# Idle matmuls in fp32, the first head group's norm taken in pieces, the second group's k moved off ScalarE, and a reordered start of the MLP, in an attention and MLP kernel

## The chip, the cores and the metric

One core of one Trainium2 chip. The metric is the time of one execution in microseconds (us), measured on the device. A profiled execution gives a trace as well. Its span is a little shorter than the timed duration (434.5 against 436.1 us for the kernel before). Stages are compared by spans, kernels by times. Each run of one core also lists the mean clock that TensorE was granted, as a share of full speed.

## The reference

Batch 8, 12 heads, 448 tokens, 64 numbers per head; then an MLP of 768 to 2048 to 768 on 3584 tokens. Everything arrives in fp32.

```python
def rmsnorm(x, g):
    return x / np.sqrt(np.mean(x * x, axis=-1, keepdims=True) + 1e-06) * g
q_n, k_n = rmsnorm(q, g_q), rmsnorm(k, g_k)
scores = np.matmul(q_n, k_n.transpose(0, 1, 3, 2)) / np.sqrt(64)
attn   = softmax(scores)                     # written out there: exp, sum, divide
x      = np.matmul(attn, v)                  # then (batch * tokens, heads * 64)
h      = x @ w_in
out    = (np.maximum(h, 0) + alpha * np.minimum(h, 0)) @ w_out
```

## The kernel before

The work is cut into 24 groups of four heads, three to a batch. The text counts groups from one; the code counts `y` from zero. A group goes through six steps:

1. `square` and `reduce` give the sums of squares, on ScalarE or GpSimd and then VectorE.
2. `root` makes the norm's factor of them, with two small operations on ScalarE.
3. `scale` multiplies q and k by the factors.
4. `turn` transposes both: on TensorE with a copy by VectorE for the first six groups (ScalarE copies the first q), by DMA later.
5. `score` makes seven tiles of scores, and `soft` takes the exponential of each on ScalarE.
6. `den` sums the exponentials over the keys on TensorE, `log` and `invert` make the reciprocal on ScalarE, `attv` multiplies with v.

Which engine does what, at the start:

```python
def square(y, nm):
    ...
    if y < 2:
        nc.scalar.activation(out=sqf, in_=src, func=AF.Square)
    else:
        nc.gpsimd.tensor_mul(out=sqf, in0=src, in1=src)

def scale(y, nm):
    ...
    eng = nc.vector if (y, nm) in ((0, "k"), (1, "q"), (2, "q"), (3, "q")) else nc.gpsimd
    eng.tensor_mul(out=..., in0=nat[y, nm], in1=...)      # rr, broadcast over a head

def spin(count):                                          # idle matmuls, fp16, 128 x 448
    if count:
        ps = psf.tile([128, 512], FP32, name="spin", tag="mm")
        for _ in range(count):
            nc.tensor.matmul(out=ps[:, :S], lhsT=ident, rhs=idle, start=True, stop=True)
```

In the traces each engine does its work in the order in which it is written here, so this order is the schedule. A "burst" is the two or three score tiles of one turn of the loop. `roots[n] = y` says after which burst the norm of group `y` is made. The burst with the second denominator is called `lead`; in it the first MLP steps (`up`) begin.

```python
spin(22)
...                                       # small transpose of the parameters
spin(6)
for nm in "qk":
    square(0, nm)
    reduce(0, nm)
...
for nm in "qk":
    root(0, nm)
    scale(0, nm)
...
turn(0)
square(1, "k")
load_v(0)
square(2, "q")
...
after(0, root, 1)
for nm in "qk":
    after(0, scale, 1, nm)
after(0, square, 2, "k")
after(0, load_w_in, 0)                    # GpSimd issues the first weights' DMAs
...
roots[3] = 2
for n in range(NB):
    ...
    if n in roots:
        y = roots[n]
        work = [(root, (y,)), (scale, (y, "q")), (scale, (y, "k"))]
        if lead:
            late = [(3, f, a) for f, a in work]       # after the third up step
        else:
            for f, a in work:
                f(*a)
    ...
    for k, (f, a) in enumerate(gaps[n]):              # the MLP steps of this burst
        ...
            f(*a, spare)
            done += 1
            if n in jobs and not (lead and done < 4):
                g, c = jobs[n].pop(0)                 # a reduce of the next group
                g(*c)
            if late and done == late[0][0]:
                for _, g, c in late:
                    g(*c)
                late = []
    ...
    if n < den_at[G - 1] - 1 and plain and n not in turns:
        spin(4)
```

## Time and profile before

| | before |
|---|---|
| time, median of 6 runs (range) | 436.12 us (435.75 to 436.34) |
| span of the profiled run, mean granted clock | 434.5 us, 0.995 |
| start of the first softmax (ScalarE) | 13.46 us |
| start of the first denominator (TensorE) | 28.40 us |
| start of the second denominator | 38.39 us |
| start of the turn of the fifth group | 52.95 us |
| start of the first down projection in a spare accumulator ("opa"), which is free only when VectorE has read the attention output of the fourth and fifth group out of it | 80.26 us |

The last five rows are milestones. They cut the span into six stages.

One more row of the page is needed later, the clock that was granted to TensorE, in tenths, 10.9 us to a digit:

```profile
PEclk9899999999999999999999999999999999999999
```

An undisturbed slice reads 9. The 8 in the second slice is one stretch of half clock, from 13.50 to 16.91 us. The record of the clock begins at 6.67 us, so the slow start before that is not in this row.

### The profile page before, as it was taken

The numbers are of one execution on the slowest core, as the hardware profiler recorded it, in microseconds if no ns is written. First come the engines' busy times: TensorE is split into PE (matmuls) and PEld (weight loads), VectorE is DVE, ScalarE is ACT, GpSimd is POOL, SyncE is SP. The second block draws the span as 40 slices with busy tenths as digits, with TensorE's granted clock in tenths as the row PEclk, the third lists the DMA queues.
The fourth block names the chain that finished last, engine by engine and source line by source line (L and its number), as shares of the span: only waits on it lengthen the run. The fifth ranks groups of instructions, "written<-read, shape, count | busy, mean of one in ns | idle before, by whom it ended". The sixth has DMA issues, their size and how long they took to land.

```text
span 434.5 us, 11509 instructions
## 1 busy us (share of the span) xinstructions
PE 417.4 (96%) x4977; PEld 215.9 (50%) x4977; DVE 204.9 (47%) x304; ACT 279.4 (64%) x385; POOL 175.8 (40%) x133
## 2 busy tenths in 40 slices
PE   7888799899999999999999999999999999999996
PEld 3344344354455445544555445554555545555564
DVE  3755564544554463546454463555453354233421
ACT  4997787588877577758757577757757587132300
POOL 5799792585373626074153636174133000000000
PEclk9899999999999999999999999999999999999999
DMA  8999999999668743968076752945082300211133
GB/s 186 234 234 218 166 210 175 201 174 189 158 104 178 170 107 62 203 101 195 20 137 156 156 129 55 200 101 121 20 150 48 80 4 21 55 38 28 28 72 75
DMA packets 70387, 53.85 MB, mean 124 GB/s; under 512 B 37424, under 2 KB 70336, under 8 KB 70336
## 3 DMA queue, kind: packets, MB, share of 16 engines
q1 hardware_dynamic: 55536, 40.19, 42.8%
q0 software_dynamic: 13984, 11.81, 18.3%
q10 hardware_dynamic: 816, 1.11, 1.1%
q8 instruction: 39, 0.64, 0.6%
q14 instruction: 12, 0.10, 0.1%
HBM read 45.62 MB, written 11.01 MB: 130 GB/s over the span
## 4 chain that ended last, share of the span: by engine, by line
PE 88%; DVE 4%; ACT 4%; issue 1%; DMA 1%; SPq 0%; ACTq 0%
PE op L364 28%; PE hT L326 21%; PE hTa L326 10%; PE sc L231 8%; PE opa L364 6%; PE dn L260 5%; PE av L260 5%; ACT expT L245 3%; PE avb L260 3%; DVE ss L153 2%; DMA nat<-in_k_dram 1%; PE tps L205 1%; DVE gT L354 1%; DVE osb L376 1%; ACT ah L353 1%
## 5 line engine op out<-in xcount | busy, mean ns | idle before, releaser
L245 ACT ACTIVATE expT<-sc,expb 128x896 f16<-128x896 f32 x168 | 161.6, 1005 | 38.8 <-PE sc L231 38.1
L364 PE MATMUL op<-w_out_sb,gT 128*128 128x384 f16 (+1 forms) x752 | 126.3, 323 | 0.0
L170 POOL TENSOR_TENSOR qs<-nat,rr 128x896 f16<-128x896 f32 x44 | 76.7, 1763 | 120.0 <-ACT rr L165 89.5
L364 PEld LDWEIGHTS <-gT 128*128 128x128 f16 x912 | 85.7, 98 | 64.8 <-issue 12.2
L326 PEld LDWEIGHTS <-w_in_sb 128*128 128x128 f16 x768 | 73.2, 98 | 74.9 <-issue 10.4
L326 PE MATMUL hT<-xT,w_in_sb 128*128 128x448 f16 x510 | 107.0, 353 | 2.0 <-DVE gT L354 2.0
L147 POOL TENSOR_TENSOR sq<-nat 128x896 f32<-128x896 f32 x44 | 73.4, 1683 | 39.9 <-DMA nat<-in_q_dram 29.1
L353 ACT ACTIVATE ah<-hT,cols 128x448 f16<-128x448 f32 x85 | 53.9, 635 | 44.0 <-PE hT L326 44.0
L354 DVE TENSOR_TENSOR gT<-hT,ah 128x448 f16<-128x448 f32 x85 | 52.8, 624 | 52.7 <-ACT ah L353 52.7
L376 DVE COPY osb<-op 128x384 f32<-128x384 f32 (+1 forms) x47 | 25.8, 549 | 90.5 <-PE op L364 90.5
L231 PE MATMUL sc<-qT,kT 64*32 64x448 f16 (+1 forms) x1092 | 54.0, 357 | 6.1 <-ACT expT L245 3.4
L153 DVE TENSOR_REDUCE ss<-sq 128x14 f32<-128x896 f32 x48 | 50.5, 1078 | 7.1 <-ACT sq L145 6.2
L326 PE MATMUL hTa<-xT,w_in_sb 128*128 128x448 f16 x246 | 53.2, 352 | 0.0
L353 ACT ACTIVATE ah<-hTa,cols 128x448 f16<-128x448 f32 x41 | 26.1, 635 | 31.2 <-PE hTa L326 31.2
L354 DVE TENSOR_TENSOR gT<-hTa,ah 128x448 f16<-128x448 f32 x41 | 25.6, 624 | 26.0 <-ACT ah L353 26.0
L231 PEld LDWEIGHTS <-kT 64*32 64x32 f16 (+1 forms) x1092 | 15.2, 93 | 37.3 <-issue 32.9
L364 PE MATMUL opa<-w_out_sb,gT 128*128 128x384 f16 x160 | 27.7, 326 | 0.0
L260 PE MATMUL dn<-expT,ones 64*32 64x448 f16 (+1 forms) x812 | 24.8, 350 | 2.6 <-issue 1.7
L311 DVE TENSOR_TENSOR xT<-av,rden 128x896 f16<-128x896 f32 x16 | 17.5, 1092 | 19.1 <-PE av L260 14.7
L260 PEld LDWEIGHTS <-vt 64*32 64x32 f16 (+1 forms) x1260 | 18.9, 94 | 13.2 <-issue 2.2
L260 PE MATMUL av<-expT,vt 64*32 64x448 f16 (+1 forms) x812 | 24.1, 349 | 0.0
L260 PEld LDWEIGHTS <-ones 64*32 64x32 f16 (+1 forms) x812 | 13.0, 94 | 12.6 <-issue 6.3
(43 smaller groups left out, 162.6 us busy)
## 6 DMA issues: line engine op xcount, KB each, us to landing
out_dram<-osb SPq DMA_DIRECT2D x109, 96.0 KB, 2.3
nat<-in_q_dram SPq DMA_DIRECT2D x46, 224.0 KB, 5.6
nat<-in_k_dram SPq DMA_DIRECT2D x46, 224.0 KB, 5.7
vt<-in_v_dram POOLq DMA_DIRECT2D x16, 336.0 KB, 6.4
w_in_sb<-in_moe_w_in_dram POOLq DMA_DIRECT2D x12, 256.0 KB, 7.4
w_out_sb<-in_moe_w_out_dram POOLq DMA_DIRECT2D x4, 768.0 KB, 11.5
nat<-in_q_dram ACTq DMA_DIRECT2D x2, 224.0 KB, 4.9
nat<-in_k_dram ACTq DMA_DIRECT2D x2, 224.0 KB, 6.3
```

What stands on the lines that cost most here:

```text
L147: nc.gpsimd.tensor_mul(out=sqf, in0=src, in1=src)
L153: nc.vector.tensor_reduce(out=ss_t[y][:, "qk".index(nm)].rearrange("p h j -> p (h j)").unsqueeze(2), in_=sqs[y, nm], axis=AXIS_X, op=ALU.add,)
L170: eng.tensor_mul(out=t.rearrange("p j h d -> p h j d"), in0=nat[y, nm], in1=rr_t[y][:, "qk".index(nm)].unsqueeze(3).broadcast_to((128, 2, ...
L231: nc.tensor.matmul(out=sc[ds(64 * g + m * c, m), par, :S].rearrange("p (j c) -> p j c", j=J), lhsT=kT[ds(64 * par, 64), j, g, ts(c, m)], r ...
L245: nc.scalar.activation(out=expT[y][:, j], in_=scs[y, j][:, :, :S], func=AF.Exp, scale=QK_SCALE, bias=expb[:, 0:1],)
L260: nc.tensor.matmul(out=accs[g][ds(m * h, m), :S], lhsT=weights(g, y, par, ts(c, m), j), rhs=expT[y][ds(64 * g, 64), j, par, :], start=(j = ...
L311: nc.vector.tensor_mul(out=x, in0=av[:, :, :S], in1=r)
L326: nc.tensor.matmul(out=hT[:, :S], lhsT=w_in_sb[:, g * G + i, ts(ft, 128)], rhs=xT[b][:, g, i, :], start=(i == 0 and g == 0), stop=(i == G ...
L353: nc.scalar.activation(out=ah, in_=hT[:, :S], func=AF.Copy, scale=alpha_sb[:, ft : ft + 1])
L354: nc.vector.tensor_max(out=gT[:, ft, ds((b & 1) * S, S)], in0=hT[:, :S], in1=ah)
L364: nc.tensor.matmul(out=ops[c][:, :PW], lhsT=gT[:, ft, ts(t, 128)], rhs=w_out_sb[:, ft, ds(oh * OH + c * PW, PW)], start=(ft == 0), stop=(f ...
L376: nc.vector.tensor_copy(out=o[:, ts(c, PW)], in_=ops[c][:, :PW])
```

## The change

The intent, part by part:

- **Idle matmuls.** They keep TensorE's clock up while it has nothing to do. Most become fp32, one wide one in place of four narrow ones, so that fewer instructions are needed.
- **First group.** q is squared, summed and scaled without waiting for k, by head halves; k is normed in two parts of its tokens (3/7 and 4/7). VectorE, not ScalarE, copies its turned q. The first softmax should start earlier.
- **Second group.** The square of its k moves from ScalarE to GpSimd, the scaling of its k from GpSimd to VectorE.
- **Third group.** Its norm is made one burst later (`roots[4]`), and on GpSimd the weights' DMA issues now stand ahead of the square of its k.
- **First MLP steps.** Both reductions of the next group go ahead of the first activation; one score tile and its softmax move behind the third and fourth `up`; the norms come after them.

The diff, cut to its core (the helpers that work on parts of the first group are left out; each is the operation of its name on a slice):

```diff
-    idle = gT[:, 0, :S]
+    idle32 = gT[:, 0, :].bitcast(FP32)
@@ square
-        if y < 2:
+        if (y, nm) == (1, "q"):
             nc.scalar.activation(out=sqf, in_=src, func=AF.Square)
@@ scale
-        eng = nc.vector if (y, nm) in ((0, "k"), (1, "q"), (2, "q"), (3, "q")) else nc.gpsimd
+        eng = nc.vector if y == 1 or nm == "q" and 0 < y <= G else nc.gpsimd
@@ spin
+                out=ps[:, :S], lhsT=idle32[:, :128] if wide else ident,
+                rhs=idle32 if wide else idle, start=True, stop=True,
@@ start
-    spin(22)
+    spin(3)
+    spin(18, False)
 ...
-    spin(6)
-    for nm in "qk":
-        square(0, nm)
-        reduce(0, nm)
+    spin(1)
+    for h in range(2):
+        part_square("q", slice(h, h + 1), full, nc.scalar)
+    for h in range(2):
+        part_reduce("q", slice(h, h + 1), full)
+    part_root("q", full)
+    part_scale("q", full, J, nc.gpsimd)
+    part_square("k", both, lo, nc.scalar)          # lo, hi: 3/7 and 4/7 of the tokens
+    part_square("k", both, hi, nc.scalar)
 ...                                                # reduce, root, turn, copy in parts
     square(1, "k")
+    reduce(1, "q")
+    square(2, "q")
     load_v(0)
-    square(2, "q")
+    after(0, part_turn, "k", range(K0, J))
+    after(0, part_copy, "k", hi, nc.vector)
+    after(0, reduce, 1, "k")
+    mid[1] = 1                                     # norm before the second burst's last softmax
     for nm in "qk":
-        reduce(1, nm)
-    after(0, root, 1)
-    for nm in "qk":
-        after(0, scale, 1, nm)
-    after(0, square, 2, "k")
-    after(0, load_w_in, 0)
+        after(1, scale, 1, nm)
+    after(1, load_w_in, 0)
+    after(1, square, 2, "k")
 ...
-    roots[3] = 2
+    roots[4] = 2
@@ loop
             if lead:
-                late = [(3, f, a) for f, a in work]
+                late = [(3, score, tiles[2]), (4, soft, tiles[2])]
+            if lead or wait and y < TD:
+                late += [(late[-1][0], f, a) for f, a in work]
 ...
-                if n in jobs and not (lead and done < 4):
+                if n in jobs:
 ...
-            spin(4)
+            spin(1)
```

## The prediction

> **What bounds the kernel now.** I read the page first, for the shares by slice; then the chain of work that ended last, in order of time; then the timeline of the first 57 us; then the table by stretches; last the waits of TensorE.
>
> ```profile
> PE   7888799899999999999999999999999999999996
> ACT  4997787588877577758757577757757587132300
> ```
>
> A slice is 10.9 us. From the sixth slice on TensorE is over 90% busy in nearly every one, and the table by stretches has it busy for 99.70 of the 100 us from 150 on. The change touches nothing after the third head group, so it can only pay in the first five slices, where TensorE is at 70 to 80%. There the chain shows who sets the pace:
>
> ```profile
> 7.51 0.96 ACT sq L145
> 8.49 1.10 DVE ss L153
> ...
> 10.20 1.44 DVE qs L170
> ...
> 11.68 0.58 PE tps L205 x7
> ...
> 12.29 0.70 DVE kT L216
> ...
> 13.46 1.91 ACT expT L245 x2
> ```
>
> The columns are start, length and work. This is a serial line from the arrival of k (7.5) to the first softmax (13.46). From then on ScalarE is nearly saturated:
>
> ```profile
> 15.78 5.67 ACT L245 ACTIVATE expT<-sc,expb 128x896 f16<-128x896 f32 x6
> 21.89 0.32 ACT L164 ACTIVATE rr<-ss,epsb 128x28 f32<-128x28 f32 x1 [0.44 <-DVE ss L153]
> 22.37 7.46 ACT L245 ACTIVATE expT<-sc,expb 128x896 f16<-128x896 f32 x8
> ```
>
> Eight softmaxes take 7.46 us (0.93 each); from 13.46 to 30.20, where the first denominator is logged, there are 16 of them (14.9) and three norms ("roots", 0.55 each): 16.6 of 16.74 us. So up to there the time is that of the first softmax plus stalls of ScalarE. A third stretch is the first MLP steps, where TensorE waits for a buffer that VectorE's reductions hold up:
>
> ```profile
> 47.94 1.07 DVE L153 TENSOR_REDUCE ss<-sq 128x14 f32<-128x896 f32 x1
> ...
> 49.60 1.29 PE L326 MATMUL hT<-xT,w_in_sb 128*128 128x448 f16 x6 [0.87 <-DVE gT L354]
> ...
> 50.58 0.32 ACT L164 ACTIVATE rr<-ss,epsb 128x28 f32<-128x28 f32 x1 [1.79 <-DVE ss L153]
> ...
> 52.63 0.38 PE L231 MATMUL sc<-qT,kT 64*64 64x448 f16 x4 [1.42 <-ACT expT L245]
> ```
>
> The brackets are idle time just before and its releaser: a reduction put between two activations delays the second (0.87 of TensorE), and ScalarE sits 1.79 us in front of the norm that needs the second reduction, so that the next softmax and scores are late (1.42).
>
> **What the Trainium skill says.** "TensorE: Matmul & The Clock Gate", Part 1 (the HAM clock gate): TensorE runs at half clock until one free-running window of about 3.4 us has been busy, and falls back after an idle one. The trace agrees: idle matmuls of 448 columns come every 0.37 us until 6.7, then every 0.19, and are back at 0.37 at 13.5 to 15.2. "FP8 and Floating Point Precision", TensorE Precision Notes: true fp32 takes four passes through the array. No line here shows it; I take one fp32 idle matmul as four fp16 ones (0.75 us, 1.5 at half clock). "SBUF — State Buffer", SBUF: two separate sides: VectorE and GpSimd share a port pair, and the one that starts second blocks for the whole instruction. The trace agrees:
>
> ```profile
> 8.99 1.69 POOL L170 TENSOR_TENSOR qs<-nat,rr 128x896 f16<-128x896 f32 x1 [4.68 <-ACT rr L165]
> 15.87 1.09 DVE L170 TENSOR_TENSOR qs<-nat,rr 128x896 f16<-128x896 f32 x1 [0.91 <-ACT rr L165]
> 15.91 2.60 POOL L170 TENSOR_TENSOR qs<-nat,rr 128x896 f16<-128x896 f32 x1 [0.56 <-ACT rr L165]
> ```
>
> The same scaling is 1.69 us alone on GpSimd, 2.60 beside one of VectorE.
>
> **The change, part by part.**
>
> *Idle matmuls.* At the start 22 + 6 narrow ones become 3 wide, 18 narrow, the small transpose, 1 wide: 30 narrow units before the transpose instead of 22. If the clock rises at 6.7 again: 14 units by then, 16 x 0.187 = 3.0, end 9.7; transpose 0.1 to 0.2 and the wide one 0.75: TensorE is free at 10.5. If it rises one or two us sooner, at about 9.7. Later bursts have one wide for four narrow: the same time.
>
> *First group.* q: two squares of 448 (0.57 each, from 0.95 for 896 with some 0.1 fixed) and two reductions follow its arrival at 5.5; sum ready at 7.2 and root at 7.8, no longer behind k's square. GpSimd scales q 7.85 to 9.54 (before 8.99 to 10.68). k: squares of 3/7 and 4/7 end 8.9, its second reduction 9.55, VectorE scales the first part 9.6 to 10.1, GpSimd the second 10.2 to 11.2. TensorE turns q at 9.7 to 10.5 and three blocks of k (0.8 together); VectorE copies q (0.62, was 0.91 on ScalarE) and 3/7 of k (0.36); scores 0.43. First softmax: 10.5 + 0.6 + 0.65 + 0.4 + 0.45 = 12.6, with the early clock 11.9. Against 13.46 that is 0.9 to 1.5 won. I take 1.2.
>
> *Second group.* k's square leaves ScalarE for GpSimd (0.95 us that lay before the first softmax, in the shadow of the turn), and both scalings run on VectorE, 2.2 in sequence, where GpSimd's blocked 2.60 ended before. Norm at about 15.2, scalings to 17.8, turns and copies to 19.2, against 19.87 before. TensorE turns k in order before it scores the next tile: about 0.3 us of stall.
>
> *Third group: its norm moves one burst later.* It now follows ten softmaxes instead of eight, but its turn stays where it was, so only two softmaxes are left between norm and first dependent tile, where there were four. Before, that tile's softmax came at 26.12, 3.65 us after the norm ended (22.47): GpSimd's blocked scaling 2.6, turn 0.55, scores 0.4. GpSimd still does this scaling and VectorE still starts beside it. So: first softmax 12.25 + 10 x 0.935 + two norms 1.1 + stall 0.3 = 23.0; + 3.65 = 26.7. ScalarE idles 3.65 - 1.9 = 1.75 us, and what was won (1.2) becomes 0.6 lost.
>
> *First MLP steps.* Both reductions go before the first activation; one score tile and its softmax move behind four activations; the norms follow. Laid out from the first matmul of hTb (41.33 now) with the durations above: reductions end at +3.7, so the first gT is no earlier (+4.3), but activations four and five then run back to back, the matmul that waited until +8.3 starts at +7.75, the norm is at +9.7 without a wait, scores at +9.7 (were +11.3) and the next up matmuls at +11.0 instead of +12.4. Won: 1.4.
>
> Sum: +0.6 - 1.4 = -0.8 us. After that both kernels run the same instructions behind a busy TensorE, so the difference stays.
>
> **Rivals.**
>
> *The late norm costs nothing.* If the square of the third group's k, now behind v's and the weights' DMA issues on GpSimd, were ready only after 22 us, the norm could not have gone earlier anyway. It doesn't alter 26.7, but if the blocked scaling shrinks to 1.69 the tile comes at 25.8 and the whole gains 1.7 us: 434.2 or less, with the early clock 433.5. Against it: three of three such pairs in the trace took 2.40 to 2.60.
>
> *The late clock.* If the window falls badly, 30 units run mostly at half clock, the first turn is at 11.4 and the first softmax at 13.4: nothing won, 0.6 + 1.2 lost at the third group, end at 436.3.
>
> *A stall outside the change.* TensorE has two idle pieces that wait for nothing shown:
>
> ```profile
> 36.06 0.57 PE L231 MATMUL sc<-qT,kT 64*64 64x448 f16 x7 [1.37 <-issue]
> ...
> 85.93 0.95 PE L260 MATMUL dn<-expT,ones 64*64 64x448 f16 x16 [1.49 <-issue]
> ```
>
> By my count of the order they lie at TensorE's 701st and 1723rd instruction, 1022 apart, and the instruction queue moves 0.64 MB, 64 bytes for each of some 9,960: I read them as instruction fetches that come late. The changed kernel has 53 fewer ahead, so they would fall in the next denominator and after; the same cost if they remain. If the first vanishes 1.4 are won (433.4); if another appears, 1.4 are lost.
>
> *All of it hidden.* That the first 57 us don't reach the end would need slack in TensorE later; 99.70 of 100 us busy speaks against it.
>
> **Range and chances.** From 435.9: -0.8 worked out, about -0.5 for the chances that the fetch stall or the blocked scaling turns out smaller, since the late norm looks like something tuned with a purpose: 434.6. The uncertainties are 0.7 (clock), 0.7 (third group), 0.5 (MLP steps) and 1.0 (fetches), together about 1.5 us; 8 times in 10 between 432.6 and 436.3. Two per cent are 8.7 us, more than any rival makes: within 2% 0.97, faster 0.02, slower 0.01.
>
> **What would show it.** First softmax at 11.9 to 12.6 in the timeline; q's scaling on GpSimd starting at 7.9; an idle piece of ScalarE of 1.5 to 1.8 us before the softmax after the third group's turn, released by scores, and GpSimd's scaling of that k at 2.6 us; the 1.79 us before the norm in the first MLP steps gone, and TensorE's waits on gT down from three to one; one fp32 idle matmul at 0.75 us at full clock. It is wrong if the first softmax is later than 13.0, if ScalarE doesn't idle at the third group, if new waits stand in the 55 to 75 us stretch, or if an issue piece of over 1 us has come or gone.

## The result, and the profile after

Ratios here and below are the mean time of one kernel's fast runs over that of the other's fast runs of the same rounds, so they are not quite the ratio of the medians quoted beside them. The bracket is a 95% interval.

| | before | after |
|---|---|---|
| time, median of 6 runs (range) | 436.12 us (435.75 to 436.34) | 440.15 us (438.43 to 441.82) |
| ratio after to before | | 1.0094 [1.0070, 1.0119] |
| profiled span, granted clock | 434.5 us, 0.995 | 438.3 us, 0.988 |

The changed kernel is 4 us slower, and above the predicted range. It is within 2%. The output is correct. The stages, each from its milestone to the next:

| stage, us | before | after | difference |
|---|---|---|---|
| 1: to the first softmax | 13.46 | 12.60 | -0.86 |
| 2: to the first denominator | 14.94 | 20.22 | +5.28 |
| 3: to the second denominator | 9.99 | 10.24 | +0.25 |
| 4: first MLP steps, to the fifth group's turn | 14.56 | 13.39 | -1.17 |
| 5: to the first opa matmul | 27.31 | 28.21 | +0.90 |
| 6: to the end | 354.24 | 353.64 | -0.60 |

Stages 1 and 4 won most of what they were meant to win. Stage 2 lost several times that, and stage 5, where nothing was changed, lost 0.9.

The page of the changed kernel, in the rows that were shown of before:

```profile
PE   8688899999999999999999999999999999999996
...
ACT  5668787677877586768657577767757578122300
...
PEclk9869999999999999999999999999999999999999
```

TensorE's second digit fell from 8 to 6, ScalarE's second and third from 99 to 66. The clock has a 6 in its third slice where before had a 9. The loss thus lies between 11 and 33 us, and a lower clock is part of it. ScalarE set the pace there, so its timeline is the ledger. The columns are start, length, work, count, and in brackets the idle time before it and what ended it. Lines have other numbers here than in the kernel before: L306 is the softmax (L245 before), L292 the scores, L165 and L166 a norm, L171 a scaling.

```profile
12.60 2.80 ACT L306 ACTIVATE expT<-sc,expb 128x896 f16<-128x896 f32 x3 [1.81 <-PE sc L292]
...
20.75 1.91 ACT L306 ACTIVATE expT<-sc,expb 128x896 f16<-128x896 f32 x2 [2.02 <-PE sc L292]
23.91 1.91 ACT L306 ACTIVATE expT<-sc,expb 128x896 f16<-128x896 f32 x2 [1.25 <-PE sc L292]
...
26.59 1.91 ACT L306 ACTIVATE expT<-sc,expb 128x896 f16<-128x896 f32 x2 [0.31 <-PE sc L292]
29.94 1.91 ACT L306 ACTIVATE expT<-sc,expb 128x896 f16<-128x896 f32 x2 [1.44 <-PE sc L292]
32.57 1.91 ACT L306 ACTIVATE expT<-sc,expb 128x896 f16<-128x896 f32 x2 [0.73 <-PE sc L292]
...
34.85 0.90 ACT L338 ACTIVATE rden<-dn 128x896 f32<-128x896 f32 x1
```

From the first softmax to the log of the first denominator there are 22.25 us (16.74 before). The brackets after the first add up to 2.02 + 1.25 + 0.31 + 1.44 + 0.73 = 5.75; the other 16.5 is work, as before. All five are released by scores, so the question is each time why TensorE was late.

**The 2.02: the second group's scalings.** VectorE's and GpSimd's timelines of the changed kernel:

```profile
16.06 3.27 DVE L171 TENSOR_TENSOR qs<-nat,rr 128x896 f16<-128x896 f32 x2 [0.64 <-ACT rr L166]
```

```profile
16.28 1.43 POOL L124 DMA_DIRECT2D w_in_sb<-in_moe_w_in_dram  x2
17.70 0.73 POOL L127 DMA_DIRECT2D w_in_sb<-in_moe_w_in_dram  x1
18.43 2.43 POOL L148 TENSOR_TENSOR sq<-nat 128x896 f32<-128x896 f32 x1
```

The second group's norm stands at 15.45 us (15.26 before): the early first softmax brought it no nearer. Its k was squared by 12.97, but the sum over it runs on VectorE only from 14.34 to 15.42, behind the copy of the first group's late part of k, which itself waits 0.84 us for TensorE. And the norm now comes after three softmaxes, where before it came after two. Then two scalings in sequence on VectorE take 3.27 us where the prediction had 2.2. One of the pair took 1.08, the other 2.26, and that one spans GpSimd's issues of the weights' DMAs. So the turn of k starts at 19.38 us; before, both turns were done by 19.13.

**The 1.25, 0.31 and 0.73: half clock.** The table by stretches, cut at the edges of the clock (columns after the window: its length, then busy time and count of TensorE, its weight loads, VectorE, ScalarE and GpSimd, then the granted clock, the DMA's share and GB/s):

```profile
16.15:19.57 3.42, 1.18 (x19) 0.69 (x15) 3.42 (x3) 2.57 (x3) 3.42 (x5) 1.00 1.17 221
19.57:26.40 6.83, 6.57 (x35) 1.98 (x32) 3.05 (x5) 4.25 (x6) 1.29 (x1) 0.50 1.19 247
26.40:29.81 3.41, 1.68 (x30) 0.93 (x22) 1.83 (x3) 1.91 (x2) 3.40 (x2) 1.00 0.46 104
29.81:33.22 3.41, 3.41 (x34) 0.89 (x34) 2.53 (x3) 2.55 (x3) 3.41 (x4) 0.50 0.82 209
```

In a stretch of 3.42 us TensorE worked 1.18 us, while it waited for the scalings, and the clock was halved for the next 6.83 us. It happened again around the third group. At half clock one fp32 idle matmul takes 1.86 us and stands in line ahead of the scores.

**The 1.44: the third group's norm,** made one burst later, with GpSimd's scaling at 2.54 us behind it.

**Stage 4.** TensorE's waits in the first MLP steps of the changed kernel:

```profile
50.20 1.29 PE L387 MATMUL hT<-xT,w_in_sb 128*128 128x448 f16 x6 [0.53 <-DVE gT L415]
...
52.83 0.38 PE L292 MATMUL sc<-qT,kT 64*64 64x448 f16 x4 [1.02 <-ACT expT L306]
```

Before there were two waits for gT (0.67 and 0.87) and one of 1.42 for the softmax, 2.96 us together; now there are 1.55. ScalarE's 1.79 us in front of the norm is gone. The stage is 1.17 us shorter.

**Stage 5.** What gives 0.9 back is a lag of GpSimd, told with the experiment that isolates it (b_lead, below).

### The profile page after: what moved, and what is told of

It is laid out like the page before. It is cut to its first block, busy times and chain, and to the rows that moved or that the text cites.

```text
span 438.3 us, 11497 instructions
## 1 busy us (share of the span) xinstructions
PE 421.0 (96%) x4965; PEld 217.1 (50%) x4965; DVE 207.0 (47%) x309; ACT 278.2 (63%) x387; POOL 176.6 (40%) x134
## 3 DMA queue, kind: packets, MB, share of 16 engines
q10 hardware_dynamic: 816, 1.11, 1.0%
## 4 chain that ended last, share of the span: by engine, by line
PE 81%; DMA 5%; DVE 4%; POOL 4%; ACT 3%; issue 3%; POOLq 0%; DVEq 0%
PE op L425 26%; PE hT L387 20%; PE hTa L387 10%; PE sc L292 7%; PE opa L425 6%; PE dn L321 4%; PE av L321 4%; PE spin L454 3%; DMA kT<-qs 3%; DMA nat<-in_k_dram 2%; PE avb L321 2%; POOL qs L171 2%; ACT expT L306 2%; DVE ss L154 2%; POOL sq L148 1%
## 5 line engine op out<-in xcount | busy, mean ns | idle before, releaser
L306 ACT ACTIVATE expT<-sc,expb 128x896 f16<-128x896 f32 x168 | 161.7, 1004 | 44.5 <-PE sc L292 43.9
L171 POOL TENSOR_TENSOR qs<-nat,rr 128x896 f16<-128x896 f32 x42 | 72.5, 1749 | 119.1 <-ACT rr L166 92.2
L148 POOL TENSOR_TENSOR sq<-nat 128x896 f32<-128x896 f32 x45 | 75.7, 1697 | 39.7 <-DMA nat<-in_q_dram 35.6
L292 PE MATMUL sc<-qT,kT 64*32 64x448 f16 (+1 forms) x1092 | 54.5, 362 | 4.5 <-ACT expT L306 2.7
L154 DVE TENSOR_REDUCE ss<-sq 128x14 f32<-128x896 f32 x46 | 48.4, 1076 | 2.7 <-POOL sq L148 2.7
L292 PEld LDWEIGHTS <-kT 64*32 64x32 f16 (+1 forms) x1092 | 14.9, 94 | 37.7 <-issue 30.2
L338 ACT ACTIVATE rden<-dn 128x896 f32<-128x896 f32 x16 | 14.5, 907 | 7.3 <-PE dn L321 7.3
```

What stands on the lines that cost most here:

```text
L154: nc.vector.tensor_reduce(out=ss_t[y][:, "qk".index(nm)].rearrange("p h j -> p (h j)").unsqueeze(2), in_=sqs[y, nm], axis=AXIS_X, op=ALU.add,)
L171: eng.tensor_mul(out=t.rearrange("p j h d -> p h j d"), in0=nat[y, nm], in1=rr_t[y][:, "qk".index(nm)].unsqueeze(3).broadcast_to((128, 2, ...
L292: nc.tensor.matmul(out=sc[ds(64 * g + m * c, m), par, :S].rearrange("p (j c) -> p j c", j=J), lhsT=kT[ds(64 * par, 64), j, g, ts(c, m)], r ...
L306: nc.scalar.activation(out=expT[y][:, j], in_=scs[y, j][:, :, :S], func=AF.Exp, scale=QK_SCALE, bias=expb[:, 0:1],)
```

## The experiments

All 17 runs gave the correct result. First comes a table: the stages of the profiled run of each kernel (columns as above), its time, and its ratio to the kernel before. The stages of a kernel are those of one trace, while the ratio comes from several runs. So stage figures show where time goes, and ratios decide. The runs were made on three chips; a ratio compares with the kernel before on the same chip, while the stages of "before" are always those of its one trace.

| kernel | 1 | 2 | 3 | 4 | 5 | 6 | median us | ratio |
|---|---|---|---|---|---|---|---|---|
| before | 13.46 | 14.94 | 9.99 | 14.56 | 27.31 | 354.24 | 436.12 | 1 |
| after | 12.60 | 20.22 | 10.24 | 13.39 | 28.21 | 353.64 | 440.15 | 1.0094 [1.0070, 1.0119] |
| a_narrow | 12.36 | 19.40 | 11.08 | 13.39 | 28.69 | 353.98 | 440.25 | 1.0111 [1.0062, 1.0160] |
| a_k1back | 12.42 | 19.80 | 10.22 | 13.39 | 29.25 | 353.52 | 439.35 | 1.0068 [1.0029, 1.0106] |
| a_root3 | 12.86 | 18.36 | 8.63 | 13.38 | 28.22 | 353.65 | 437.46 | 1.0031 [1.0012, 1.0049] |
| b_lead | 13.54 | 14.93 | 10.08 | 13.39 | 28.65 | 354.61 | 437.34 | 1.0029 [1.0005, 1.0053] |
| b_lead2 | 13.20 | 14.91 | 11.70 | 13.52 | 27.31 | 353.76 | 435.43 | 0.9986 [0.9967, 1.0005] |
| a_win | 12.27 | 20.10 | 10.45 | 13.39 | 29.14 | 353.75 | 441.09 | 1.0109 [1.0087, 1.0131] |
| a_nospin | 12.62 | 19.20 | 10.63 | 13.39 | 29.26 | 354.70 | 440.80 | 1.0108 [1.0091, 1.0125] |
| b_first | 12.12 | 18.20 | 10.88 | 14.54 | 27.32 | 353.84 | 439.31 | 1.0075 [1.0041, 1.0110] |
| a_warm | 12.50 | 18.44 | 12.52 | 13.39 | 28.55 | 353.70 | 443.04 | 1.0153 [1.0098, 1.0208] |
| a_all | 12.50 | 18.29 | 9.16 | 13.33 | 27.62 | 353.10 | 436.57 | 1.0005 [0.9977, 1.0033] |
| b_first2 | 12.35 | 15.88 | 10.07 | 14.55 | 27.31 | 353.94 | 436.92 | 1.0019 [0.9997, 1.0041] |
| b_best | 12.80 | 15.95 | 10.24 | 13.33 | 27.31 | 354.07 | 437.00 | 1.0023 [1.0007, 1.0040] |
| a_fix | 13.03 | 18.05 | 11.53 | 14.18 | 27.39 | 353.32 | 438.33 | 1.0059 [1.0035, 1.0083] |
| b_lead2_again | 13.36 | 14.91 | 9.91 | 13.33 | 27.30 | 353.79 | 434.90 | 0.9990 [0.9973, 1.0008] |
| b_norm2 | 12.61 | 15.23 | 12.07 | 14.55 | 27.30 | 353.84 | 436.00 | 1.0000 [0.9983, 1.0016] |
| b_norm2_lead | 12.08 | 14.97 | 9.66 | 13.33 | 27.31 | 353.25 | 434.74 | 0.9965 [0.9945, 0.9986] |
| a_norm2 | 13.00 | 18.62 | 10.73 | 13.39 | 28.48 | 353.98 | 439.43 | 1.0057 [1.0028, 1.0086] |

A name with a_ starts from the changed kernel, one with b_ from the kernel before. The first four runs split the change.

### a_narrow: the idle matmuls narrow and fp16 again

```diff
-    spin(3)
-    spin(18, False)
+    spin(22, False)
 ...
-    spin(1)
+    spin(6, False)
 ...
-            spin(1)
+            spin(4, False)
```

> The changed kernel with every idle matmul narrow in fp16 again (22, 6 and 4 as before the change). Theory 'the port' (the cascade starts where VectorE's two scalings of the second group and GpSimd's DMA issues share a port: 3.27 us instead of 2.2, ScalarE idle 2.02 us, TensorE starved and thrown to half clock): the stall of 2.0 us before the second group's first softmax stays, and the half clock after it stays at least in part; time 438.5 to 440.5. Theory 'fp32' (wide idle matmuls are what loses the clock and blocks the scores, 1.86 us each at half clock): no half clock between 19 and 33 us, ScalarE's idle pieces of 1.25 and 0.73 us gone, time 437 to 438. First softmax 0.3 to 0.6 us earlier in both, as the start has 8 narrow units less.

Measured: 440.25 us, no faster than the changed kernel. Stage 2 is 0.8 shorter in this trace, stage 3 is 0.8 longer, with a stall of 2.32 us that waits for nothing shown (see the end of this part). So the fp32 form is not what the loss rests on; a share like the 0.8 us of stage 2 is not excluded.

### a_k1back: the second group's k squared on ScalarE and scaled on GpSimd again

```diff
-        if (y, nm) == (1, "q"):
+        if y == 1:
 ...
-        eng = nc.vector if y == 1 or nm == "q" and 0 < y <= G else nc.gpsimd
+        eng = nc.vector if nm == "q" and 0 < y <= G else nc.gpsimd
```

> The changed kernel with the second group's k squared on ScalarE and scaled on GpSimd as before. Theory 'the port': VectorE's one scaling takes 1.09 us again, GpSimd's 2.6, the turn of k comes at about 18.6 instead of 19.4, ScalarE's idle piece before the second group falls from 2.0 to about 1.2 or less, TensorE idles less and may keep its clock; time 437 to 438.5. Theory 'fp32': the clock falls as in the changed kernel, idle pieces of 1.2 and 0.7 us behind wide idle matmuls stay; time 439 to 440.

Measured: 439.35 us; the interval of its ratio overlaps that of the changed kernel. The wait at the second group shrank from 2.02 to 1.53 us, and the two half-clock waits behind it stayed (1.25 and 0.78). So the two scalings are a part, and not the largest.

### a_root3: the third group's norm one burst earlier, as before

```diff
-    roots[4] = 2
+    roots[3] = 2
```

> The changed kernel with the third group's norm one burst earlier, where it was before the change. Theory 'late norm': ScalarE's idle piece of 1.44 us at the third group's first softmax goes, but the norm itself now waits for the sum of squares, which is ready at 22.9 in the changed kernel, about 0.3 us after the eighth softmax; net 1 us won, 439. Rival: the pace there is set by TensorE at half clock, so nothing is won, 440.

Measured: 437.46 us, about two thirds of the loss gone, by one index. Stage 2 is 1.9 shorter: the norm is made at 23.53 us instead of 25.70, and the 1.44 is gone. Stage 3 is 1.6 shorter than in the changed kernel, mostly because its stall of 1.27 us does not appear in this trace. That second part is not owed to the norm in any way that a trace shows.

### b_lead: the kernel before with nothing but the reordered first MLP steps

The edit is the part "@@ loop" of the diff above, applied to the kernel before, without the idle matmuls.

> The kernel before with the one part of the change that reorders the first MLP steps (both reductions ahead of the activations, one score tile and its softmax behind them, norms later), nothing else. If the parts add up: 1.2 us won as in the changed kernel (delay 4.8 us at the second denominator, 3.6 at the turn of the fifth group), 434.8 us. Rival: the 1.2 us there was only catching up of a late start, nothing won, 436.0.

Measured: 437.34 us, slower than before. Stage 4 won 1.17 us as it should. Stage 5 lost 1.34. The lines that show why are two from the kernel before (GpSimd's scalings of the fourth group; the transposed k of the seventh, which arrives by DMA and is multiplied by VectorE):

```profile
46.59 3.33 POOL L170 TENSOR_TENSOR qs<-nat,rr 128x896 f16<-128x896 f32 x2 [2.73 <-ACT rr L165]
```

```profile
77.75 0.45 DVE L191 TENSOR_SCALAR kT<-kT,gain 128x896 f16<-128x896 f16 x1 [0.85 <-DMA kT<-qs]
```

and the same two from b_lead:

```profile
48.82 3.33 POOL L170 TENSOR_TENSOR qs<-nat,rr 128x896 f16<-128x896 f32 x2 [4.92 <-ACT rr L165]
```

```profile
79.08 0.45 DVE L191 TENSOR_SCALAR kT<-kT,gain 128x896 f16<-128x896 f16 x1 [3.19 <-DMA kT<-qs]
```

Because the fourth group's norm now comes after a softmax (48.16 us on ScalarE, 45.90 before), GpSimd starts its scalings 2.23 us later. GpSimd then works almost without a pause until about 70 us, so the delay travels with it. The seventh group's k is transposed by a DMA that is issued at 70.30 us (68.07 before) and lands at 79.06 us, 1.33 us later than before (77.73). VectorE takes its work in order, so it waits 3.19 us for this k (0.85 before), and behind it waits the multiplication that frees the accumulator which TensorE needs for opa. The lag of an engine that was off the path came due 30 us later.

### b_lead2: b_lead with the fourth group's norm ahead of the score tile and softmax

```diff
             if lead:
-                late = [(3, score, tiles[2]), (4, soft, tiles[2])]
-            if lead or wait and y < TD:
+                late = [(3, f, a) for f, a in work]
+                late += [(3, score, tiles[2]), (4, soft, tiles[2])]
+            elif wait and y < TD:
                 late += [(late[-1][0], f, a) for f, a in work]
```

> The kernel before with the reordered first MLP steps of the run b_lead, but with the fourth group's norm put back ahead of the fourth activation. In b_lead 1.0 us was won by the turn of the fifth group and 1.3 lost at 84 us, where VectorE waited 3.2 us for the seventh group's transposed k. Theory 'GpSimd's lag': the loss comes from the norm that ScalarE did 2.2 us later, which GpSimd, busy from there to 68 us, carried to the transposes; with the norm early the scalings start near 46.6 again, VectorE's wait falls to about 1, the 1.0 us stays: 435.0 us. Rival: the transposes are slow for another reason (loads beside them) and the loss stays: 436.5 or more.

Measured: 435.43 us. Stage 5 is back at 27.31, stage 4 keeps 1.04 of its gain. This trace lost 1.7 us in stage 3: its stall was 1.63 us (1.37 before), and a stretch of half clock (36.77 to 40.18) followed. The traced run of b_lead2_again, below, had no such stretch.

### a_win: the third group's k squared ahead of the weights' DMA issues

```diff
-    after(1, load_w_in, 0)
     after(1, square, 2, "k")
+    after(1, load_w_in, 0)
```

> The changed kernel with GpSimd's square of the third group's k ahead of the first weights' DMA issues instead of behind them; no other edit. Theory 'the port': VectorE's two scalings of the second group take 1.1 to 1.7 instead of 2.3 and 1.1 us, the second ends about 1 us sooner, ScalarE's idle 2.0 us falls to about 1, the sum of the third group's k comes 2 us sooner; time 438 to 439.5. Rival: GpSimd's square holds the same port for 1.7 us and the scalings end as late as now, 440.

Measured: 441.09 us, no gain. One of VectorE's scalings now ran beside GpSimd's square and took 2.71 us; the wait at the second group was 2.05. The neighbour changed, the price did not. The earlier square is of no use either while the norm stays in its late place.

### a_nospin: no idle matmuls between the bursts

```diff
-            spin(1)
+            pass
```

> The changed kernel without the idle matmuls between the bursts (those at the start stay). Theory 'idle matmuls in the way': at half clock each wide one holds TensorE 1.86 us in front of scores that ScalarE waits for (idle 1.25, 0.31 and 0.73 us); without them these go, the first denominator comes 1.5 to 2 us sooner; time 438 to 439. Rival 'clock': without them half clock lasts through the denominator and the values (three runs of 1.5 us become 3), what is won is lost again, 440 to 442.

Measured: 440.80 us. The idle matmuls no longer stand in front of the scores, and the waits of 1.25 and 0.73 us are gone: the softmaxes run four in a row. But TensorE was at half clock from 16.19 to 36.67 us. The third group's wait grew to 2.43 us, and the first denominator took 2.81 us (1.52 at full clock). The gain is lost in another place: the idle matmuls are in the way, and they are needed.

### b_first: the kernel before with the split of the first group

The first group's parts of the diff, with narrow idle matmuls, `roots[3]`, the second group's k as before, and the MLP steps as before. GpSimd's order is still that of the changed kernel.

> The kernel before with the one part of the change that splits the first group (q squared and summed by heads, k in two token parts, second group's norm after the third softmax); idle matmuls narrow, second group's k squared on ScalarE and scaled on GpSimd, third group's norm and the MLP steps as before the change. If the earlier first softmax (12.4 instead of 13.46) carries through: 435.0 us. Rival: TensorE starves at the second group and falls to half clock as in all runs with this start so far: 436.5 to 437.5.

Measured: 439.31 us, slower by 3 us although the first softmax started 1.3 us earlier. Stages 4 to 6 are those of the kernel before; stage 2 lost 3.3 us, and stage 3 0.9 with a stall of 2.12 us (1.37 before). ScalarE's line in b_first:

```profile
23.08 0.32 ACT L165 ACTIVATE rr<-ss,epsb 128x28 f32<-128x28 f32 x1 [2.13 <-DVE ss L154]
```

This is the third group's norm. It waits 2.13 us for a sum, because GpSimd issued the weights' DMAs ahead of the square (square at 20.21 us; 18.33 in b_first2). The change's later norm may have been meant as a way around this order of GpSimd's.

### a_warm: two wide idle matmuls ahead of the turns of the second and third group

```diff
         if not gaps[n] and n in turns:
+            if turns[n] < G:
+                spin(2)
             turn(turns[n])
```

> The changed kernel with two wide idle matmuls more ahead of each of the turns of the second and third group, where TensorE sat idle before it fell to half clock. Theory 'clock': full clock from 6 us on, wide idle matmuls 1.0 us instead of 1.86, ScalarE's idle pieces of 1.25, 0.31 and 0.73 us mostly gone, less 0.5 us for the later turn; first denominator 1.5 us sooner; 438.5 us. Rival: the pace is set by the scalings and norms alone, the extra idle matmuls only delay the turns: 440 to 441.

Measured: 443.04 us, the slowest of all, and yet stage 2 did what was wanted. From 5.72 us the clock was full until 39.86 us, and of the waits of 1.25, 0.31 and 0.73 only 0.20 was left, so stage 2 is 1.8 us shorter. Stage 3 took that back. TensorE's timeline of a_warm:

```profile
39.72 0.49 PE L292 MATMUL sc<-qT,kT 64*64 64x448 f16 x3 [2.01 <-issue]
40.15 3.17 PE L387 MATMUL hT<-xT,w_in_sb 128*128 128x448 f16 x8
```

A stall that waits for nothing shown took 2.01 us, and in the stretch from 36.44 to 39.86 us TensorE worked only 1.29 us. The clock was halved for the next 3.41 us, so eight matmuls took 3.17 us (1.69 in the kernel before). In this trace stage 3 is 2.5 us longer than before. The range of its four timed runs is wide, 440.02 to 445.22, and only the first of them was traced.

### a_all: the changed kernel with both norms in their early places

a_root3 and b_lead2's edit together.

> The changed kernel with two of its moves undone together: third group's norm where it was before the change, fourth group's norm ahead of the fourth activation. If the causes add (2.7 us by the first alone, 1.9 us by the second between b_lead and b_lead2): 435.5 to 436.0. Rival: with the third group's norm early GpSimd isn't late any more and the second has nothing to win: 437.4.

Measured: 436.57 us, ratio 1.0005: parity with the kernel before. Two moved norms undo the loss on average. Part of this may be luck: the trace has no stall over 0.7 us in stage 3, worth about 1 us against the kernel before (0.36 against 1.37 us), and nothing shows that the norms cause that.

### b_first2: b_first with GpSimd's order as before

```diff
     reduce(1, "q")
-    square(2, "q")
     load_v(0)
+    square(2, "q")
 ...
-    after(1, load_w_in, 0)
     after(1, square, 2, "k")
+    after(1, load_w_in, 0)
```

> The run b_first with GpSimd's queue in the order of the kernel before (v's DMA issues, square of the third group's q, scaling of the second group's k, square of the third group's k, then the first weights' issues). In b_first ScalarE sat 2.13 us before the third group's norm, whose sum was late by these issues. Theory 'GpSimd's order': that wait falls to 0.5 or less and the early first softmax carries through at last: 435.3 us. Rival: TensorE still starves and falls to half clock: 437 or more.

Measured: 436.92 us, not told apart from before. Stage 2 is 2.3 us shorter than in b_first, by an exchange of two pairs of lines in one queue. ScalarE's lines:

```profile
19.35 1.91 ACT L306 ACTIVATE expT<-sc,expb 128x896 f16<-128x896 f32 x2 [0.97 <-PE sc L292]
21.73 0.32 ACT L165 ACTIVATE rr<-ss,epsb 128x28 f32<-128x28 f32 x1 [0.47 <-DVE ss L154]
```

The first softmax is 1.11 us earlier than before, and 0.94 of it is lost again in stage 2, to 0.97 us of waiting at the second group. Its norm came at 15.11, no sooner than before. So even with a full clock (no stretch below it in this trace) the start that was won was worth only 0.17 us at the first denominator. What held the norm is tested by the last three runs.

### b_best: b_first2 with b_lead2's MLP steps

> The parts that seemed to pay, together: first group split, GpSimd's queue as before the change, idle matmuls narrow, second group's k squared on ScalarE and scaled on GpSimd, third group's norm early, reordered MLP steps with the fourth group's norm ahead of the fourth activation. If they add up: b_first2 less 0.7, 434.5 us or less, faster than both kernels. Rival: equal to the kernel before.

Measured: 437.00 us, slightly slower than before, though the traced run was 0.8 us shorter in span (433.7). The sum of two parts that each seemed good or neutral is not better than before.

### a_fix: a_all with a_warm's idle matmuls

> The run a_all (third group's norm early, fourth group's norm ahead of the fourth activation) with the extra idle matmuls of a_warm. At the first denominator the changed kernel is 4.4 us behind the kernel before; the early norm alone took 1.6 of it (a_root3), the full clock alone 1.9 (a_warm). Theory 'two separate causes': they add, the first denominator is 0.5 to 1.3 us behind and no half clock stands before it; the end at 435.0 to 436.0 if the idle piece at TensorE's 701st instruction is no longer than 1.5 us. Rival 'one cause': half clock follows from the late norm, the extra idle matmuls win nothing more than a_all, first denominator 2.4 behind.

This run was to show whether the late norm and the lost clock add up. Measured: 438.33 us over eight runs. Stage 2 is 18.05 us. With the early norm alone (a_root3, a_all) it was 18.36 and 18.29; with the full clock alone (a_warm) 18.44; with neither 20.22. The two together win what each wins alone. So they are not two separate losses of 2 us that can be taken back one after the other; ahead of both lies the second group, with a wait that neither edit touches. ScalarE waits 1.49 us there, then 0.52 for the third group's norm and 1.49 for its scores. In b_first2, whose stage 2 is 15.88, these are 0.97, 0.47 and none. b_first2 differs in GpSimd's order, in the idle matmuls and in the second group's k, and no run says how the 2.2 us between them are shared. In stage 3 a stall of 1.84 us and half clock from 40.93 to 44.34 followed again, as in a_warm.

### b_lead2_again: b_lead2 once more, with more rounds

> The kernel of the run b_lead2 once more, unchanged, in five rounds, as its interval (0.9967 to 1.0005) left open whether it beats the kernel before. If the 1.0 us of the MLP steps is real: ratio 0.9985 or lower with the interval below 1. Rival: equal, interval around 1.

Measured: 434.90 us median of 22 runs, before 436.06 of 29 runs of the same rounds, ratio 0.9990 [0.9973, 1.0008]. Stage 4 won 1.23 us, and stage 5 kept it. VectorE's line:

```profile
76.59 0.45 DVE L191 TENSOR_SCALAR kT<-kT,gain 128x896 f16<-128x896 f16 x1 [1.14 <-DMA kT<-qs]
```

It waits 1.14 us for the seventh group's k, not 3.19. The runs fall into two heaps by granted clock. Sixteen with a clock of 0.996 or more lie between 433.79 and 435.65 us; six below it between 436.77 and 438.72. The medians differ by 1.2 us in its favour, but the interval holds 1, so it is not shown to be faster. Choosing the runs with the better clock would be choosing the answer.

### b_norm2: b_first2 with the second group's norm unblocked

```diff
+    after(0, reduce, 1, "k")
     after(0, part_copy, "k", hi, nc.vector)
-    after(0, reduce, 1, "k")
-    mid[1] = 1                                # norm after three softmaxes
+    after(0, root, 1)                         # norm after two
```

> The split of the first group with GpSimd's order as before, and in addition the second group's second reduction put ahead of the copy of the first group's late part of k on VectorE, its norm after two softmaxes instead of three. Theory A (the time won at the first softmax is absorbed because VectorE's order makes the second group's reduction wait for the copy of the first group's late k, and the norm's place makes it wait for a third softmax): the norm of the second group starts at 14.1 to 14.4 us instead of 15.11, the wait of ScalarE at the second group falls from 0.97 to under 0.5, and the first denominator starts at 27.5 to 27.9 (28.23 without the edit). Theory B (the arrival of the second group's k and the blocked scaling on GpSimd set the pace): the norm comes sooner, but GpSimd's scaling waits for the square of the third group's q until 15.2 and is blocked as before; first denominator at 28.1 to 28.4, no gain. Third possibility: the late copy of the first group's k delays the first group's fourth tile, a new wait of 0.3 us.

Measured: theory A in the stages. The norm came at 14.38 us, the wait at the second group fell to 0.42, the first denominator started at 27.84:

```profile
18.97 1.90 ACT L306 ACTIVATE expT<-sc,expb 128x896 f16<-128x896 f32 x2 [0.42 <-PE sc L292]
```

Of the 0.85 us that the first softmax had won in this trace, 0.56 reached the first denominator (0.17 of 1.11 in b_first2). So the place of one reduction and one norm had kept most of the won start from being passed on. The time is 436.00 us over 22 runs, ratio 1.0000: the trace gave the gain away in stage 3, with a stall of 2.01 us and eight matmuls in 2.73 us (1.69 before).

### b_norm2_lead: b_norm2 with b_lead2's MLP steps

> The same with the reordered first MLP steps and the fourth group's norm ahead of the score tile. If both parts add up and theory A holds: 1.2 us won in the MLP steps and 0.6 at the first denominator, time 434.2 to 434.8 against 436.1, ratio about 0.996. Theory B: 434.9 to 435.5. If clock and stall interfere as in earlier combinations: 436 to 437.5.

Measured: 434.74 us over 22 runs (432.43 to 438.29), ratio 0.9965 with an interval below 1. It is the only version here that is shown to be faster than the kernel before, by 0.35%, and so faster than the changed kernel too. It differs from b_best (1.0023) by that one edit. ScalarE's timeline in its trace, which is its fastest run:

```profile
13.87 0.31 ACT L165 ACTIVATE rr<-ss,epsb 128x28 f32<-128x28 f32 x1
14.22 0.23 ACT L166 ACTIVATE rr<-rr 128x28 f32<-128x28 f32 x1
14.35 5.72 ACT L306 ACTIVATE expT<-sc,expb 128x896 f16<-128x896 f32 x6
```

Six softmaxes in a row and no bracket: the wait at the second group is gone. Stage 2 is as long as before (14.97 and 14.94) from a first softmax that is 1.38 us earlier, and the two gains of the change, 1.38 and 1.23, are both kept in this trace. The median time is only 1.2 us below that of the kernel before, so most runs keep less; they were not traced.

### a_norm2: the changed kernel with the same edit

> The changed kernel with that one edit. Theory A: the second group's norm at 14.3 to 14.6 instead of 15.45, its two scalings partly ahead of the weights' DMA issues, the 2.02 us wait down to 1.0 to 1.3, and with the shorter wait perhaps no half clock at the second group; stage from first softmax to first denominator 18 to 19.2 instead of 20.2, time 438 to 439.5. Theory B: one scaling is blocked by the weights' issues all the same and ends no sooner than 19.0; wait 1.8 to 2.1, time 439.5 to 441.

Measured: 439.43 us, ratio 1.0057 [1.0028, 1.0086] (1.0094 without the edit; the intervals overlap). The norm came at 14.80 us, the first of the five waits fell from 2.02 to 1.01 us, and stage 2 to 18.62. The scalings took 3.58 us all the same, one of them beside the weights' issues, and the third group's norm is still late (a wait of 1.86 us).

### A stall that came along in most traces

In 16 of the 19 traces TensorE stands still for 1.04 to 2.32 us, waiting for nothing shown, at its 701st recorded instruction, whatever that instruction is. In the changed kernel that is:

```profile
42.18 0.74 PE L387 MATMUL hT<-xT,w_in_sb 128*128 128x448 f16 x3 [1.27 <-issue]
```

Before, it is the 1.37 us that the prediction shows, in a score matmul. A transfer of 16 KB on the instruction queue starts 0.2 to 1.5 us before the stall, and TensorE goes on 2.3 to 2.8 us after the start of that transfer, in all 16. In a_root3, a_nospin and a_all there was no stall over 0.7 us; there the transfer had started 2.0 to 2.9 us before the instruction was due. So the stall is as long as the transfer is late. A second one, at the 1723rd instruction, behaves alike: ten traces have it, with 0.76 to 1.50 us, and TensorE goes on 2.6 to 2.9 us after the transfer's start; in the nine without it the transfer had started 3.3 us or more ahead. That these are late instruction fetches fits well; no run moved a transfer to prove it, and what sets the start of a transfer is open.

## Why the prediction was wrong

**Right, at the edge of its range: the first softmax.** Predicted 12.25 us, 0.9 to 1.5 us won; measured 12.60, 0.86 won. GpSimd's scaling of q started at 7.74 us (7.85 predicted).

**Right: one fp32 idle matmul costs about what four narrow ones do.** One took 1.02 us between bursts at full clock and 1.86 us at half; four narrow ones 0.93 and 1.67. The prediction's 0.75 us is a pace from start to start, while these lengths include the modelled end of the last; like for like the miss is about 0.1 us, and a_narrow is no faster.

**Wrong: "about 0.3 us of stall" at the second group.** This is the first step that failed. It was 2.02 us. The prediction had the norm at about 15.2 us and the scalings done at 17.8. The norm came at 15.45, and one scaling of the pair took 2.26 us beside GpSimd's issues of the weights' DMAs, which the prediction had counted as free. The deeper mistake: the prediction carried the 1.2 us of the first softmax through to the third group, with a norm that it itself put no earlier than before. b_first2 shows the gain absorbed in front of that norm (0.94 of 1.11 us), and b_norm2 and b_norm2_lead show why: VectorE's order and a third softmax held the norm. With these two moved, most of it passes through (0.56 of 0.85 us in b_norm2, 1.35 of 1.38 in b_norm2_lead).

**Wrong: the clock was reckoned only at the start.** The prediction's rival "the late clock" asks whether the first 30 idle matmuls raise it in time. It did not ask whether the longer waits at the second and third group would lower it again. They did: 10.24 us at half clock in two stretches (before: one stretch of 3.41), and ScalarE idle for 1.25 + 0.31 + 0.73 us behind it. The prediction counted on a fall after an idle window only; the trace shows one after a stretch that was a third busy. Its own trace had shown this, and it read it as agreeing: before the half clock at 13.50 us, TensorE had worked 1.68 of 3.41 us (10.09 to 13.50), 1.12 of it turns.

**Right in mechanism and size: the third group's late norm.** Predicted 3.65 us from the end of the norm to the dependent softmax, with 1.75 us of idle ScalarE in them; found 3.66 (26.28 to 29.94), with 0.31 + 1.44 = 1.75 us idle and GpSimd's scaling at 2.54. That scores at half clock made 0.31 of it was not foreseen, but it didn't lengthen this path. a_root3 takes it back and wins the most of all single edits. But a_fix shows that this loss and that of the clock overlap, so the 5.75 us of the ledger can't be split into causes that add up. Of the rivals, "the late norm costs nothing" is refuted by a_root3. Its condition did hold: with GpSimd's new order the square was ready late, and the norm at its early place waited 0.27 us for it (2.13 in b_first), but even so it came 2.2 us sooner.

**Right: the first MLP steps.** Predicted 1.4 us won, measured 1.17 in stage 4 of the changed kernel and again in b_lead. TensorE's waits on gT went from three (0.67, 0.87 and 0.42 us) to two (0.53 and 0.42), not to one.

**Wrong: "so the difference stays" after them.** 0.9 us was given back in the changed kernel in stage 5, 1.34 in b_lead. The prediction held that "the change touches nothing after the third head group", yet it moves the norm of the fourth. It watched TensorE and ScalarE there; the delay travelled on GpSimd, through a DMA, to VectorE. Across the table, stage 5 is 27.3 to 27.6 us in each kernel with the fourth group's norm in its early place (before, b_lead2 twice, b_first, b_first2, b_best, b_norm2, b_norm2_lead, a_fix, a_all) and 28.2 to 29.3 in each with the late one. From opa on the claim holds: stage 6 is 353.1 to 354.7 us in all 19 traces.

**The rival of a stall outside the change** cost nothing either way between these two traces: at the 701st instruction both have one, 1.37 us before and 1.27 after. Only its place was predicted wrongly; it fell in the first MLP matmuls, not in the denominator. The second piece that it named (1.49 us at 85.93) is gone in the changed kernel, one of the prediction's own signs of being wrong. It is absent in each of the nine kernels with the fourth group's norm late, and present in each of the ten with it early. This decided nothing either: stage 6, in which it lies, is 353.5 to 354.7 us without it and 353.1 to 354.2 with it.

**"All of it hidden"** is refuted: opa starts 4.4 us later, and 3.8 us of that reach the end.

**The sum.** Predicted +0.6 at the third group and -1.4 at the MLP, -0.8 in all. Found -0.86 + 5.28 + 0.25 - 1.17 + 0.90 - 0.60 = +3.8 us of span, +4.0 of time. The class (within 2%) was right, as no part of a 57 us stretch could reach 8.7 us.

**Open.** How stage 2's loss is shared between scalings, clock and late norm has no single answer, as they overlap. What sets the start of the transfer behind stage 3's stall, and whether half clock follows, was not found; it moves single traces by as much as the edits do.

## What to carry to other kernels

Time won ahead of a chain is worth only as much as the next thing that the chain waits for allows: look for that second pacer before moving work. Moving a norm, a reduction or a DMA issue by one place in an in-order queue can cost 2 us in that queue, or 30 us later at the end of another engine's backlog, so follow every queue that the move delays and not only the one that was short of time. On TensorE a wait of one or two us (1.02 in the changed kernel, 2.01 in a_warm) also risks the clock: 6.83 and 3.41 us at half clock followed, which slowed everything queued behind it.

## What the Trainium skill lacked or had wrong

- "TensorE: Matmul & The Clock Gate", "Why this matters for your kernels", advises no idle gaps over about 3 us between bursts. Here the clock was halved after a stretch in which TensorE worked 1.18 of 3.42 us with no single gap over 1.02 us, and after one with 1.68 of 3.41 us, of which 1.12 were transposes (Part 4 of that page says that these don't count as busy in the same way). In a_warm 1.29 of 3.42 us, with one gap of 2.01, did it too. The length of the half-clock stretches, 3.41 us or a multiple of it (6.83, and 20.48 in a_nospin), agrees with Part 1. How busy a window has to be is on no page, and these runs don't fix it.
- "SBUF — State Buffer", "SBUF: two separate sides", tells of GpSimd's descriptor writing being held up by VectorE. The other direction is missing: a two-input scaling on VectorE took 2.26 us (changed kernel) and 2.57 us (a_root3) beside GpSimd's issue of the weights' DMAs, and 1.09 alone or, in a_k1back, with these issues out of its way. The issue of v's DMAs had no such effect (1.09 in a_narrow). Why the two differ is not shown.
- "Runtime: NRT & Kernel Launch", "Instruction fetch mechanics", has the cost of crossing a 16 KiB block of instructions mostly hidden. Here TensorE stood still for 1.04 to 2.32 us at its 701st instruction in 16 of 19 traces, and went on 2.3 to 2.8 us after the start of a 16 KB instruction transfer. The page doesn't say when a block comes too late. That the stall is such a block is not proved.
- "FP8 and Floating Point Precision", "TensorE Precision Notes", gives four passes for fp32, and the time agrees (1.02 us against 0.93 for four fp16 matmuls). It doesn't say that the profile records such a matmul as two.
